# The opening of an attention and MLP kernel: products and turns in pairs of 128x64 tiles, one copy for x's second half, w_out's fields earlier

## The chip, the cores and the metric

The kernel runs on one core of a Trainium2 chip. The metric is the device time of one execution in microseconds (us). The time before is the median of three runs.

## The reference

Two blocks in a row, all in float32:

```
q_p, k_p = phi(q), phi(k)            # phi(x)[i, j] = (S1 x)[i] * (S2 x)[j], 8 x 8 features of 32 dimensions
kv = sum over tokens of k_p * v;  z = sum over tokens of k_p
x  = (q_p kv) / (q_p z + 1e-6)       # 4 batches, 4 heads, 1088 tokens, head_dim 32
x  -> (4 * 1088, 128)                # the heads of a token side by side
out = gelu(x @ w_in) @ w_out         # w_in 128 x 2048, w_out 2048 x 128, exact gelu
```

S1, S2, w_in and w_out arrive as 64-bit words. The kernel takes each apart into a low word, a mantissa field and an exponent field, and puts a float32 together from them (the class `Rounding`).

## The kernel before, in words

The 4352 tokens are taken in eight chunks of 512 (`n` = 0 to 7, two to a batch) and one of the 256 left over (`n` = 8). For each chunk there is `xT[n]`, the attention output with the 128 channels on partitions and the tokens along the row. `hidden(n, fi)` multiplies one 128-column tile of w_in with `xT[n]` into a PSUM bank (512 columns), and ScalarE applies gelu to it. There are 16 such steps for each chunk. `project(n, fi)` multiplies a gelu tile with a tile of w_out and sums in PSUM. Most chunks are projected by `two_products` instead, a scheme of seven products for eight on quarter tiles, in which two products of 64 output columns always stand side by side.

A float32 matmul is two passes in the trace, each with a weight load. The page writes the tile shape as rows*columns: 128*128 is the whole array, 128*64 one half of its columns. Two 128*64 instructions on the two halves run at the same time.

The instructions of each engine run in the order of the text: a loop at the end of the kernel makes each instruction follow the one before it on its engine. So a wait holds up all that stands behind it on that engine.

The opening, up to the first steps, is written out by hand. Chunk 0 takes x by token: `divide` (VectorE, L738) makes `x_tok` in two halves of 256 tokens, and each half is turned into `xT[0]` by TensorE against `ident` and then copied out of PSUM. The first half goes through `turn_half` (two transposes at L759 and one ScalarE copy at L760), the second through `turn_half_apart` (two transposes at L751 into two banks, one copied by ScalarE and one by VectorE, both L753). Between the two, TensorE makes one factor of chunk 1's query features (`expand_products`, L579). Then `first_hidden` starts the first products of chunk 0 by columns, as the parts of `xT[0]` come (L794). In the first four steps TensorE runs `hidden(0, 0)` to `hidden(0, 3)` (L778), the products of chunk 1's ratio (`ratio_products`, L688) and the projections of chunk 0 (L965), while VectorE and ScalarE unfold w_in's second piece and w_out's first two pieces, multiply chunk 1's features (`expand_copy` L585 on ScalarE, `expand_multiply` L590 on VectorE) and make `xT[1]` (`ratio`, L707 and L708). At step 4 `first_hidden(1, half)` starts chunk 1.

`Rounding` for one piece of weights has these parts: `fields` (VectorE: exponent field L283, mantissa field L288), `low_words` (ScalarE, L270), `exponents` (ScalarE, L294, needs the exponent field), `mantissas` (VectorE, L302, needs mantissa field and low words), `signs` (VectorE, L307, needs the exponents), `product` (L312). `finish` is mantissas, signs and product.

Two PSUM banks serve `hidden_bank` and two serve `out_bank`, each given out in turn. `hidden(n, fi)` splits its tile into two halves of 64 columns only from step 17 on (`by_halves=t >= 17`); up to there it and `project` use the whole array.

Of the kernel before, what the change touches and what calls it, by code (L numbers as in the profile page):

```python
# [8 lines left out]
FP = mybir.dt.float32  # L9
# [7 lines left out]
def kernel(  # L17
# [18 lines left out]
    pe, dve, act, pool, sp = nc.tensor, nc.vector, nc.scalar, nc.gpsimd, nc.sync  # L36
# [11 lines left out]
    CW = JC * 128  # L48
# [13 lines left out]
    att = ctx.enter_context(tc.tile_pool(name="att", bufs=2))  # L62
# [5 lines left out]
    def work_banks():  # L68

        return wps.tile([128, 2, CW], FP, name="w_ps")  # L70
# [7 lines left out]
    def hidden_bank():  # L78
        return hps.tile([128, CW], FP, name="h_ps")

    def out_bank():
        return ops.tile([128, CW], FP, name="o_ps")


    by_act, by_dve, by_pool = act.copy, dve.tensor_copy, pool.tensor_copy
# [11 lines left out]
    w_in_sb = [big.tile([d_model, c1 - c0], FP, name=f"w_in{i}") for i, (c0, c1) in enumerate(pieces)]  # L97
    w_out_sb = [big.tile([128, c1 - c0], FP, name=f"w_out{i}") for i, (c0, c1) in enumerate(pieces)]
# [42 lines left out]
    def block(dtype=U32):  # L141

        b = big.tile([128, NB, 512], U32, name="block", bufs=3)
        return b if dtype == U32 else b.bitcast(dtype)
# [82 lines left out]
    ident = big.tile([128, 128], FP, name="ident")  # L227
# [318 lines left out]
    qT, qp, xT = {}, {}, {}  # L546
# [36 lines left out]
    def expand_copy(n, i):  # L583
        A[i] = att.tile([128, 2, CW // 2], FP, name="A_sb")
        act.copy(out=A[i][:, :, :width[n] // 2], in_=B_of[n, i][:, :, :width[n] // 2])  # L585

    def expand_multiply(n, i):
        W = width[n]
        a, b = (t.rearrange("f g (r x) -> f g r x", r=2) for t in (A[i][:, :, :W // 2], B_of[n, i][:, :, W // 2:W]))
        dve.tensor_mul(out=qp[n].rearrange("f r (g x) -> f g r x", g=G)[:, 2 * i:2 * i + 2], in0=a, in1=b)  # L590
# [90 lines left out]
    def ratio_products(n, banks):  # L681

        for s in range(2):
            for c in range(NP):
                rows = slice(c * F, (c + 1) * F)
                for r in range(2):
                    for i, (h, w) in enumerate(((2 * c + r, kz_apart[rows, r, c, :D]), (2 * (1 - c) + r, z_cols[rows, r]))):
                        pe.matmul(banks[h * D:(h + 1) * D, i, s * HW:(s + 1) * HW], lhsT=w,  # L688
                                  rhs=qp[n][rows, r, s * HW:(s + 1) * HW], start=True, stop=True)
# [20 lines left out]
    x_tok = {}  # L710
# [33 lines left out]
        act.activation(out=den[:, 0], in_=by_head(bank)[:, :, D], func=ACT.Copy, bias=1e-6)  # L744
        return den

    def turn_half_apart(n, i, banks):
        if i == 0:
            xT[n] = att.tile([128, CW], FP, name="xT", bufs=3)
        for j, ps in enumerate(banks):  # L750
            pe.transpose(ps[:, :128], in_=x_tok[n, i][:, j].rearrange("p h d -> p (h d)"), identity=ident)  # L751
        for j, ps in enumerate(banks):
            (by_act, by_dve)[j](out=xT[n][:, i * 256 + j * 128:i * 256 + (j + 1) * 128], in_=ps[:, :128])  # L753

    def turn_half(n, i, ps, copy):
        if i == 0:
            xT[n] = att.tile([128, CW], FP, name="xT", bufs=3)
        for j in range(2):
            pe.transpose(ps[:, j * 128:(j + 1) * 128], in_=x_tok[n, i][:, j].rearrange("p h d -> p (h d)"), identity=ident)  # L759
        copy(out=xT[n][:, i * 256:(i + 1) * 256], in_=ps[:, :256])  # L760


    g_of, o_of = {}, {}

    def w_tile(w, fi):
        i = max(i for i, (c0, c1) in enumerate(pieces) if c0 <= fi * 128)
        at = fi * 128 - CUTS[i]
        return w[i][:, at:at + 128]

    first_banks, begun = {}, [(0, 0), (1, 0)]  # L770

    def hidden(n, fi, by_halves=False):
        W = width[n]
        ps = first_banks.pop((n, fi)) if (n, fi) in first_banks else hidden_bank()
        w = w_tile(w_in_sb, fi)
        for rows in (slice(0, 64), slice(64, 128)) if by_halves else (slice(0, 128),):
            if (n, fi) not in begun:
                pe.matmul(ps[rows, :W], lhsT=w[:, rows], rhs=xT[n][:, :W], start=True, stop=True)  # L778
        if n < NCH and fi < USUAL[n]:
            g_of[n, fi] = mlp.tile([128, CW], FP, name="g", bufs=4)  # L780
        else:
            if fi % NB == 0:
                blocks[n, fi // NB] = block(FP)
            g_of[n, fi] = blocks[n, fi // NB][:, fi % NB]
        act.activation(out=g_of[n, fi][:, :W], in_=ps[:, :W], func=ACT.Gelu)  # L785

    def first_hidden(n, half):

        if half == 0:
            first_banks[n, 0] = hidden_bank()  # L790
        parts = 1 if n else 2
        for i in range(parts):
            cols = slice(half * 256 + i * 256 // parts, half * 256 + (i + 1) * 256 // parts)
            pe.matmul(first_banks[n, 0][:, cols], lhsT=w_tile(w_in_sb, 0), rhs=xT[n][:, cols], start=True, stop=True)  # L794

# [154 lines left out]
    def project(n, fi, parts=range(B // 2), cols=slice(None)):  # L952
        first, final = fi == (BLOCKED if n == NMAIN else 0), fi == (USUAL[n] if n < NCH else NF) - 1
        if first and n not in o_of:
            o_of[n] = out_bank() if n < NMAIN else [out_bank() for i in range(B // 2)]
        g = g_of[n, fi]
        if n == NMAIN:

            for i in parts:
                for half in range(2):  # L960
                    rows, at = slice(half * 64, (half + 1) * 64), i * 128 + half * 64
                    pe.matmul(o_of[n][i][rows, :128], lhsT=g[:, at:at + 64], rhs=w_tile(w_out_sb, fi),  # L962
                              start=first, stop=final)
            return
        pe.matmul(o_of[n][:, cols], lhsT=w_tile(w_out_sb, fi), rhs=g[:, cols], start=first, stop=final)  # L965

    def store(n):
        oT = mlp.tile([128, JC, d_model], FP, name="oT")
# [42 lines left out]
    banks = [out_bank(), out_bank()]  # L1011
# [26 lines left out]
    for c in range(NP):  # L1038
        rows = slice(c * F, (c + 1) * F)
# [5 lines left out]
    w_out = [Rounding(w, beside=b) for w, b in zip(w_out_sb[:2], w_in)]  # L1045
    parts = [range(2), range(2, JC)]
# [10 lines left out]
    divide(0, nd[1:], 1, den)  # L1057
    expand_products(1, (1,))
    w_in[1].fields()
    turn_half_apart(0, 1, [out_bank(), out_bank()])  # L1060
    w_in[1].exponents()
    w_in[1].mantissas()
    w_in[1].signs()
    w_in[1].product()
    expand_copy(1, 0)
# [100 lines left out]
    def begin(w):  # L1166

        rounding[w.name] = Rounding(w)
        rounding[w.name].fields()
# [51 lines left out]
    for n in range(3, NCHUNK):  # L1221

        t = (n - 1) * NF
# [75 lines left out]
    for t in range(len(steps) + LAG):  # L1299
        if t < 4:  # L1300

            hidden(0, t)
            if t == 0:
                expand_multiply(1, 0)
                w_out[0].fields()
                expand_copy(1, 1)
                expand_multiply(1, 1)
            if t == 1:
                w_out[0].low_words()
                w_out[0].exponents()  # L1310
                w_out[0].finish()
                w_out[1].fields()
            if t == 2:
                w_out[1].low_words()
            if t == 3:
                banks = work_banks()
                ratio_products(1, banks)
                w_out[1].mantissas()
                w_out[1].exponents()
                w_out[1].signs()  # L1320
                w_out[1].product()
                turned = ratio_turn(banks)
                ratio(1, banks, turned)
                project(0, 0)
                project(0, 1)
            continue
        if t == 4:
            begin(turns[0])
            by_scalar(turns[0], *low)
            for f, *a in products[t] + products[t + 1]:  # L1330
                f(*a)
            for half in range(2):
                first_hidden(1, half)
        for n in drains[t]:
            drain(n)
        sooner = t == NMAIN * NF
        if sooner:
            for f, *a in products[t]:
                f(*a)
        if t < len(steps):  # L1340
            n, fi = steps[t]
            hidden(n, fi, by_halves=t >= 17)
        if t < len(steps) and steps[t][0] < NMAIN and steps[t][1] % NB == NB - 1:
            n, b = steps[t][0], steps[t][1] // NB
            if b >= first_block(n):
                token_sums(n, b)
        for f in slots[t]:
            f()
        for n in done[t]:
            store(n)  # L1350
        if t not in (4, 5) and not sooner:
            for f, *a in products[t]:
                f(*a)
# [41 lines left out]
```

## Time and profile before

| | |
|---|---|
| time, median of 3 runs | 257.62 us (257.45 to 257.73) |
| the profiled execution's own time | 257.87 us |
| its span, first to last instruction | 256.1 us |
| PE busy | 252.0 us (98%) |
| VectorE (DVE) busy | 158.0 us (62%) |
| ScalarE (ACT) busy | 113.7 us (44%) |
| GpSimd (POOL) busy | 176.0 us (69%) |
| `hidden`, L778 | 538 instructions, 137.0 us busy, of them 30 in the shape 128*128 |
| `project`, L965 | 24 instructions, 11.9 us busy |
| granted TensorE clock | 1.000 |

The span is that of one profiled execution, and all starts and durations below come from it. A busy time is the union of the instructions of a group, and the mean of a matmul is longer than the distance from one to the next, since matmuls overlap in the array. In the chain of work that ended last each piece is put down to what released the next one, followed back from the last instruction. In a timeline the columns are start and duration in us, engine, line, operation, output and inputs, shape and count, and in brackets the engine's idle time before it and what ended that.

### The profile page before, as it was taken

The numbers are of one execution on the slowest core, as the hardware profiler recorded it, in microseconds if no ns is written. First come the engines' busy times: TensorE is split into PE (matmuls) and PEld (weight loads), VectorE is DVE, ScalarE is ACT, GpSimd is POOL, SyncE is SP. The second block draws the span as 40 slices with busy tenths as digits, with TensorE's granted clock in tenths as the row PEclk, the third lists the DMA queues.
The fourth block names the chain that finished last, engine by engine and source line by source line (L and its number), as shares of the span: only waits on it lengthen the run. The fifth ranks groups of instructions, "written<-read, shape, count | busy, mean of one in ns | idle before, by whom it ended". The sixth has DMA issues, their size and how long they took to land.

```text
span 256.1 us, 6035 instructions
## 1 busy us (share of the span) xinstructions
PE 252.0 (98%) x2444; PEld 131.3 (51%) x2444; DVE 158.0 (62%) x333; ACT 113.7 (44%) x220; POOL 176.0 (69%) x193
## 2 busy tenths in 40 slices
PE   8999999999999999999999999999999999999994
PEld 4844444455454545454444455455544444445784
DVE  3899996949798987580178986299507000700282
ACT  3683885333535333533335332533444333532541
POOL 3516019999849787587758775787758777877960
PEclk9999999999999999999999999999999999999999
DMA  6699658710001101102000002000110200020021
GB/s 207 174 298 314 183 123 211 183 19 7 0 3 15 26 4 26 18 10 33 3 0 0 0 13 33 4 1 0 19 25 3 42 0 3 3 40 0 0 33 33
DMA packets 29083, 13.50 MB, mean 53 GB/s; under 512 B 21888, under 2 KB 27264, under 8 KB 29056
## 3 DMA queue, kind: packets, MB, share of 16 engines
q1 hardware_dynamic: 28624, 12.79, 20.4%
q8 instruction: 19, 0.31, 0.6%
q10 hardware_dynamic: 432, 0.33, 0.4%
q14 instruction: 8, 0.07, 0.1%
HBM read 10.88 MB, written 2.23 MB: 51 GB/s over the span
## 4 chain that ended last, share of the span: by engine, by line
PE 95%; DVE 3%; issue 0%; ACT 0%; DVEq 0%
PE h_ps L778 44%; PE o_ps L864 35%; PE o_ps L965 3%; PE w_ps L934 2%; PE w_ps L463 1%; PE w_ps L613 1%; PE w_ps L668 1%; PE w_ps L997 1%; PE w_ps L579 1%; PE h_ps L348 1%; PE o_ps L962 1%; PE o_ps L452 1%; PE w_ps L1084 1%; DVE bits_m L302 0%; DVE bits_e L307 0%; DVE q_pT L590 0%
## 5 line engine op out<-in xcount | busy, mean ns | idle before, releaser
L778 PE MATMUL h_ps<-xT,w_in 128*64 128x512 f32 (+2 forms) x538 | 137.0, 568 | 0.0
L785 ACT ACTIVATE block<-h_ps 128x512 f32<-128x512 f32 (+1 forms) x132 | 75.4, 572 | 119.0 <-PE h_ps L778 115.9
L864 PE MATMUL o_ps<-block,w_out 128*64 128x256 f32 x232 | 59.5, 379 | 0.0
L829 POOL TENSOR_TENSOR bits_low<-block 128x512 f32<-128x512 f32 x29 | 37.3, 1288 | 28.3 <-ACT block L785 28.3
L778 PEld LDWEIGHTS h_ps<-xT,w_in 128*64 128x64 f32 (+1 forms) x538 | 40.7, 140 | 27.1 <-issue 7.8
L864 PEld LDWEIGHTS o_ps<-block,w_out 128*64 128x64 f32 x232 | 31.7, 137 | 39.2 <-issue 28.0
L830 POOL TENSOR_TENSOR bits_a<-block 128x512 f32<-128x512 f32 x29 | 37.0, 1277 | 11.7 <-ACT block L785 11.6
L879 DVE COPY sums<-o_ps 64x256 f32<-64x256 f32 x8 | 3.3, 417 | 58.9 <-PE o_ps L864 58.9
L831 POOL TENSOR_TENSOR bits_e<-bits_a,block 128x512 f32<-128x512 f32 x29 | 37.4, 1288 | 2.3
L832 POOL TENSOR_TENSOR bits_m<-block,bits_e 128x512 f32<-128x512 f32 x29 | 37.3, 1286 | 2.3
L864 PE MATMUL o_ps<-bits_low,small 128*64 128x256 f32 x116 | 29.8, 380 | 0.0
L864 PE MATMUL o_ps<-block,small 128*64 128x256 f32 x116 | 29.8, 380 | 0.0
L864 PE MATMUL o_ps<-bits_a,small 128*64 128x256 f32 x116 | 29.8, 379 | 0.0
L864 PE MATMUL o_ps<-bits_m,w_out 128*64 128x256 f32 x116 | 29.8, 379 | 0.0
L864 PEld LDWEIGHTS o_ps<-block,small 128*64 128x64 f32 x116 | 15.7, 137 | 18.7 <-issue 10.9
L864 PE MATMUL o_ps<-bits_e,small 128*64 128x256 f32 x116 | 17.7, 384 | 0.0
L864 PEld LDWEIGHTS o_ps<-bits_m,w_out 128*64 128x64 f32 x116 | 15.9, 137 | 0.0
L864 PEld LDWEIGHTS o_ps<-bits_a,small 128*64 128x64 f32 x116 | 15.8, 137 | 0.0
L864 PEld LDWEIGHTS o_ps<-bits_low,small 128*64 128x64 f32 x116 | 15.7, 137 | 0.0
L625 DVE STREAM_TRANSPOSE w_ps<-w_ps 128x512 f32<-128x512 f32 (+1 forms) x7 | 4.8, 687 | 17.1 <-ACT xT L679 12.7
L864 PEld LDWEIGHTS o_ps<-bits_e,small 128*64 128x64 f32 x116 | 7.8, 137 | 11.5 <-issue 9.1
L1108 DVE TENSOR_REDUCE w_ps<-k_p 128x128 f32<-128x1024 f32 x6 | 11.9, 1977 | 0.2
(222 smaller groups left out, 317.6 us busy)
## 6 DMA issues: line engine op xcount, KB each, us to landing
block<-in_moe_w_in_dram SPq DMA_DIRECT2D x3, 512.0 KB, 9.7
block<-in_moe_w_out_dram SPq DMA_DIRECT2D x3, 512.0 KB, 10.1
k<-in_k_dram SPq DMA_DIRECT2D x12, 128.0 KB, 2.7
v<-in_v_dram SPq DMA_DIRECT2D x12, 128.0 KB, 3.3
q<-in_q_dram SPq DMA_DIRECT2D x24, 64.0 KB, 2.6
out_dram<-oT SPq DMA_DIRECT2D x21, 64.0 KB, 2.3
q_first<-in_q_dram SPq DMA_DIRECT2D x2, 256.0 KB, 3.9
v<-in_v_dram SPq DMA_DIRECT2D x2, 256.0 KB, 4.2
```

Of the source, the lines that this page charges most:

```text
L625: dve.transpose(out=tok, in_=ps[:, :, :H2])
L778: pe.matmul(ps[rows, :W], lhsT=w[:, rows], rhs=xT[n][:, :W], start=True, stop=True)
L785: act.activation(out=g_of[n, fi][:, :W], in_=ps[:, :W], func=ACT.Gelu)
L829: pool.tensor_sub(out=s[3], in0=a11, in1=a21)
L830: pool.tensor_add(out=s[1], in0=a21, in1=a22)
L831: pool.tensor_sub(out=s[2], in0=s[1], in1=a11)
L832: pool.tensor_sub(out=s[4], in0=a12, in1=s[2])
L864: pe.matmul(acc[n][bank][half * 64:(half + 1) * 64, col:col + HW], lhsT=fixed, rhs=moving, start=opens and e == 0 and name in "4715", stop ...
L879: dve.tensor_copy(out=N[lo, 0, one], in_=a0[lo, one])
L934: pe.matmul(acc[NMAIN][rows, COLS_REM[name]], lhsT=tokens[:, rows], rhs=fixed, start=k == 0 and name == ORDER_REM[0], stop=k == BLOCKED // ...
L965: pe.matmul(o_of[n][:, cols], lhsT=w_tile(w_out_sb, fi), rhs=g[:, cols], start=first, stop=final)
L1108: dve.tensor_reduce(out=sums[:, c], in_=k_p[b][c].rearrange("p n r f -> p (r f) n"), axis=mybir.AxisListType.X, op=AX.add)
```

## The change

Four edits, all in the opening:

- Every `hidden`, `first_hidden` and `project` works on two halves of 64 columns (`sides`), also before step 17. `first_hidden(0, half)` has one piece of 256 columns in place of two of 128.
- The turns of `x_tok` are no longer transposes: `turn_x` multiplies each half of 64 columns of x with `ident`, as an ordinary product.
- x's second half is turned into one bank and copied once, by ScalarE. The VectorE copy and one `out_bank` go.
- `w_out[0].low_words()` (ScalarE) stands ahead of that turn, and `w_out[0].fields()` (VectorE) between the mantissas and the signs of `w_in[1]`. Before, they stood in steps 1 and 0.

```diff
-    def turn_half_apart(n, i, banks):
-        if i == 0:
-            xT[n] = att.tile([128, CW], FP, name="xT", bufs=3)
-        for j, ps in enumerate(banks):
-            pe.transpose(ps[:, :128], in_=x_tok[n, i][:, j].rearrange("p h d -> p (h d)"), identity=ident)
-        for j, ps in enumerate(banks):
-            (by_act, by_dve)[j](out=xT[n][:, i * 256 + j * 128:i * 256 + (j + 1) * 128], in_=ps[:, :128])
-
     def turn_half(n, i, ps, copy):
         if i == 0:
             xT[n] = att.tile([128, CW], FP, name="xT", bufs=3)
         for j in range(2):
-            pe.transpose(ps[:, j * 128:(j + 1) * 128], in_=x_tok[n, i][:, j].rearrange("p h d -> p (h d)"), identity=ident)
+            turn_x(ps[:, j * 128:(j + 1) * 128], x_tok[n, i][:, j])
         copy(out=xT[n][:, i * 256:(i + 1) * 256], in_=ps[:, :256])
...
+    sides = (slice(0, 64), slice(64, 128))
+
+    def turn_x(to, x):
+        x = x.rearrange("p h d -> p (h d)")
+        for rows in sides:
+            pe.matmul(to[rows], lhsT=x[:, rows], rhs=ident, start=True, stop=True)
+
-    def hidden(n, fi, by_halves=False):
+    def hidden(n, fi):
...
-        for rows in (slice(0, 64), slice(64, 128)) if by_halves else (slice(0, 128),):
+        for rows in sides:
...
-        parts = 1 if n else 2
-        for i in range(parts):
-            cols = slice(half * 256 + i * 256 // parts, half * 256 + (i + 1) * 256 // parts)
-            pe.matmul(first_banks[n, 0][:, cols], lhsT=w_tile(w_in_sb, 0), rhs=xT[n][:, cols], start=True, stop=True)
+        cols = slice(half * 256, (half + 1) * 256)
+        for rows in sides:
+            pe.matmul(first_banks[n, 0][rows, cols], lhsT=w_tile(w_in_sb, 0)[:, rows], rhs=xT[n][:, cols], start=True, stop=True)
...
-        pe.matmul(o_of[n][:, cols], lhsT=w_tile(w_out_sb, fi), rhs=g[:, cols], start=first, stop=final)
+        for rows in sides:
+            pe.matmul(o_of[n][rows, cols], lhsT=w_tile(w_out_sb, fi)[:, rows], rhs=g[:, cols], start=first, stop=final)
...
     w_in[1].fields()
-    turn_half_apart(0, 1, [out_bank(), out_bank()])
+    w_out[0].low_words()
+    turn_half(0, 1, out_bank(), by_act)
     w_in[1].exponents()
     w_in[1].mantissas()
+    w_out[0].fields()
     w_in[1].signs()
     w_in[1].product()
...
             if t == 0:
                 expand_multiply(1, 0)
-                w_out[0].fields()
                 expand_copy(1, 1)
                 expand_multiply(1, 1)
             if t == 1:
-                w_out[0].low_words()
                 w_out[0].exponents()
                 w_out[0].finish()
                 w_out[1].fields()
```

In the order of each engine's instructions the change moves nothing else: GpSimd's and SyncE's orders stay as they were.

More of the change, by code (lines that the diff above doesn't have):

```diff
@@ L959, in project @@
             for i in parts:
[L960 to L963, printed above, removed]
+                tokens = g[:, i * 128:(i + 1) * 128]
+                for rows in sides:
+                    pe.matmul(o_of[n][i][rows, :128], lhsT=tokens[:, rows], rhs=w_tile(w_out_sb, fi), start=first, stop=final)
             return
-        pe.matmul(o_of[n][:, cols], lhsT=w_tile(w_out_sb, fi), rhs=g[:, cols], start=first, stop=final)
+        for rows in sides:
+            pe.matmul(o_of[n][rows, cols], lhsT=w_tile(w_out_sb, fi)[:, rows], rhs=g[:, cols], start=first, stop=final)
     def store(n):
@@ L1341 @@
             n, fi = steps[t]
-            hidden(n, fi, by_halves=t >= 17)
+            hidden(n, fi)
         if t < len(steps) and steps[t][0] < NMAIN and steps[t][1] % NB == NB - 1:
```

## The prediction

> **What bounds the kernel now.** I read the page first, its chain of work that ended last:
>
> ```profile
> ## 4 chain that ended last, share of the span: by engine, by line
> PE 95%; DVE 3%; issue 0%; ACT 0%; DVEq 0%
> ```
>
> The chain is TensorE nearly throughout, and 3% is VectorE. The same chain in order of time, from 13 to 25 us, shows where that 3% lies:
>
> ```profile
> 13.55 0.37 PE h_ps L759 x2
> 13.91 0.62 PE w_ps L579 x16
> 14.53 0.27 PE o_ps L751
> 14.80 0.02 issue
> 14.83 0.27 ACT xT L753
> 15.10 0.05 issue
> 15.15 0.41 DVE bits_m L302
> ...
> 23.56 0.44 DVE xT L708
> 24.00 0.04 issue
> 24.04 0.70 PE h_ps L794 x2
> ```
>
> From 14.8 to 24.0 us the path is VectorE: it unfolds the weights and then makes the second chunk's xT (L708). TensorE resumes the path at 24.04 with `first_hidden(1, 1)`. After that I compared the starts of successive products in the trace: from 24.6 us to the last product at 252.6 us only 2.2 us are lost, nearly all in steps of about 0.09 where the tile shape changes, none of them a wait that the first 40 us set. So the change counts in two places: when VectorE finishes xT, and how fast TensorE goes from there to 42 us, where the old kernel uses pairs already. The timelines of the engines give the prices:
>
> ```profile
> 13.48 0.44 PE L759 MATMUL h_ps<-ident,x_tok 128*128 128x128 f32 x2
> 13.85 0.69 PE L579 MATMUL w_ps<-qT,Srep 32*64 32x256 f32 x16
> 42.52 0.44 PE L421 MATMUL w_ps<-ident,k_rem 128*64 128x128 f32 x4
> 42.79 1.03 PE L778 MATMUL h_ps<-xT,w_in 128*64 128x512 f32 x4
> ...
> 13.95 0.37 ACT L760 COPY xT<-h_ps 128x256 f32<-128x256 f32 x1 [0.52 <-PE h_ps L759]
> 14.83 0.27 ACT L753 COPY xT<-o_ps 128x128 f32<-128x128 f32 x1 [0.50 <-PE o_ps L751]
> 14.99 0.51 ACT L294 ACTIVATE bits_r<-bits_e,below 128x256 uint32<-128x256 uint32 x1
> ...
> 14.94 0.29 DVE L753 COPY xT<-o_ps 128x128 f32<-128x128 f32 x1
> ...
> 15.53 0.43 DVE L307 SCALAR_TENSOR_TENSOR bits_e<-small,bits_r 128x256 uint32<-128x256 uint32 x1
> ```
>
> The reader is to see that two turns by transpose hold TensorE for 0.37 (13.48 to 13.85), that one turn by two 64-column products (L421) holds it for 0.27, and that VectorE's `signs` (L307, 15.53) starts 0.03 after ScalarE's exponents (L294) end at 15.50: that edge is tight already.
>
> **The products in pairs.** A full 512-column product takes 0.857 (L778 and L965 alternate at 27.25, 28.10, 28.96); a pair takes the same (L778 128*64: 42.79 and the next instruction 0.86 later). The 20 products between 24.6 and 42 us (17.3 / 0.857) therefore gain and lose nothing. A pair gains only where TensorE has stood still: its first pass is 0.53 long in the 128-column form (0.107 of weight load exposed, 19.60 to 20.13) and 0.05 shorter with 64 columns (L421's first pass takes 0.16, its second 0.11). Most such places lie beside VectorE's path. On the path it is `first_hidden(1, 1)`, -0.05. Behind it `hidden(1, 2)` waits 0.10 today for gelu(1, 0) to free its bank; in pairs that gelu would end near 25.63 and TensorE be through with `hidden(1, 1)` at 25.69, so the wait goes as well. Together -0.13, rounded down because the two starts nearly coincide. `first_hidden(0, ...)` needs four pair passes of 0.216 for eight of 0.111, and is not on the path.
>
> **The turns as products.** L421's four instructions are one turn, two passes of each half side by side; a second turn adds 0.21 (L493: four instructions from 59.59 to 59.80). Two turns stream for 0.27 + 0.21 = 0.48, and 0.1 goes to the change of shape behind them, 0.58 against 0.37: +0.21. There are two such pairs in series on TensorE (L759, then L579, then L751), and L751 starts when L579 is through (14.46, x_tok was ready at 14.29), so the second starts at 14.68 and its last pass, begun 0.38 later, ends 0.27 after that, at 15.34. Before, the first bank was ready at 14.79, the other at 14.90.
>
> **The copy of x's second half.** One 256-element copy by ScalarE instead of 128 by each engine. It waits for all of the turn: start 15.37, 0.37 long by L760, and the next instruction follows 0.27 after its start (0.16 behind the 128 one). VectorE loses L753: it holds 0.21 of its time (14.94 to 15.15). But the exponents stand behind this copy in ScalarE's order: they start at 15.64 rather than 14.99 and end at 16.15 rather than 15.50. VectorE's `signs` waits for them and starts at 16.19 instead of 15.53, +0.66; behind it wait the w_in product and the two L590.
>
> **w_out's fields and low words.** The fields (L283 and L288, 0.20 each) leave the place between the two L590 and run while VectorE now waits for the exponents, so 0.40 of the 0.66 comes back; without that cover they would cost as before. The low words (L270, 0.44) go into ScalarE's wait ahead of the second copy (idle 0.50 before L753, longer now), cost nothing there, and leave the stretch at 17.34. Their data landed at 13.54, before either asks.
>
> **The sum.** `signs` 16.19, w_in product 16.65, first L590 16.99, second L590 17.59 by VectorE's own order. ScalarE sets nearly the same: exponents 15.64, A copy 16.06, gelu(0, 0) 16.54 (its product ends at 16.45), second A copy 17.03 to 17.61, hence second L590 at 17.65, against 17.34: +0.31. All behind it is one queue of VectorE, so xT is ready at 24.30 for 23.99. With -0.13 on TensorE the span grows by 0.18: 256.1 + 0.2 = 256.3. The profiled execution took 257.87 for a span of 256.1, 0.25 over the median of the runs, so against the median: 257.62 + 0.18 = 257.8.
>
> Bounds of the disputed term, the turn: no dearer than the transposes (0.37), the exponents would end at 15.72, the second L590 would start near 17.15 and the sum be -0.3; if the halves of a turn ran one after the other, eight passes of 0.11, each pair of turns costs 0.65 more than now, `signs` slips to about 17.1 and the sum is +1.0. L421 and L493 are the same operation on another tile, so I stay near them.
>
> The Trainium skill, "TensorEngine Tiling (Array Packing)", Restrictions, says that column tiling does without the transpose mode for FP32, and "TensorE: Matmul & The Clock Gate", Terms, calls that mode four times faster for FP32. By the four, an estimate, the two turns would stream for some 0.87 and the sum be near +1.0; by L421 and L493 the ratio is two, and the trace speaks against the four.
>
> **Rivals.**
> - *TensorE's own queue takes VectorE's place (slower).* The gelus slip with the copy: gelu(0, 1) ends at 18.11 for 17.47 in my sum, `hidden(0, 3)` waits for its bank, and behind it stand the ratio products and eight passes of L965 (19.60 to 23.14 before, to 23.67 after), then `first_hidden(1, 0)` to 24.10. xT is due at 24.35 on TensorE. It decides once gelu(0, 1) ends 0.25 later than I have it, and if ScalarE's five instructions before it slip by 0.6 the sum is about +0.55. For it: ScalarE is without a gap from 14.8 to 20; against it: the low words have left that stretch.
> - *The turns run at a fourth of the speed (slower):* +1.0, as above.
> - *The wait does not bite (faster).* If the turns are as quick as before, VectorE keeps the 0.21 of L753 and TensorE its 0.13: -0.3. For it: the chain is VectorE's and an instruction leaves it; against it: L421's four instructions for a transpose's one.
> - *Nothing of it counts:* 0.0, if VectorE had slack ahead of 24.04. The chain shows none.
>
> **How the numbers follow.** About 0.2% (0.5 us) is what a measurement of this kernel can tell from no change. My forecast, +0.2, has 0.60 and its own range is -0.1 to +0.5; TensorE's queue 0.16, the slow turns 0.07, the faster case 0.14, nothing 0.03. Slower by over 0.2%: most of the queue case (0.12), the slow turns (0.07), a tail of the forecast (0.03), 0.22. Faster by over 0.2%: only the far end of the faster case and what I may have priced wrongly in the pairs, 0.08. The rest is 0.70. The range goes from the faster case, 257.62 - 0.4 = 257.2, to most of the slower ones, 257.62 + 0.9 = 258.5.
>
> **What would show it.** In the profile after: the second turn's eight instructions from about 14.7, ScalarE's one copy at 15.4, exponents at 15.6, VectorE idle about 0.5 before `signs` at 16.2, the two L590 0.6 apart, xT's last half near 24.3, first project after it near 26.6 (26.39 before), and from there the same distance to the end. I am wrong if `signs` starts before 15.7, if pairs take other than 0.86, or if TensorE rather than VectorE precedes 24.3.

## The result, and the profile after

The changed kernel takes 258.14 us (median of 12 runs, 257.66 to 258.56), the kernel before in the same session 257.52 us (12 runs, 257.04 to 257.78). The ratio is 1.0025 (95% interval 1.0015 to 1.0034): 0.6 us slower, where 0.2 was forecast. 257.8 was the forecast time, in a range of 257.2 to 258.5; the range holds the time, but 0.70 stood on "within 0.2%" and 0.22 on "slower by more", and it was slower by a little more. The opening went nearly as it was forecast, 0.29 us slower for 0.18. A second cost came on top, 130 us later, which no step of the forecast had.

The chain of work of the changed kernel, in order of time; the columns are start, length and what:

```profile
13.51 0.59 PE h_ps L769 x8
14.10 0.62 PE w_ps L579 x16
14.71 0.61 PE o_ps L769 x8
15.33 0.02 issue
15.35 0.37 ACT xT L752
15.72 0.42 ACT bits_r L294
16.14 0.02 issue
16.16 0.44 DVE bits_e L307
...
23.85 0.44 DVE xT L708
24.28 0.04 issue
24.33 0.65 PE h_ps L792 x4
```

Before, the chain went from the turn to VectorE within 0.6 us (L751, a copy, L302). Now it runs through the longer turn, ScalarE's copy (L752) and ScalarE's exponents (L294), and reaches VectorE at its `signs` (L307). VectorE's own timeline shows what that does to it:

```profile
15.29 0.29 DVE L283 TENSOR_SCALAR bits_e<-small 128x256 uint32<-128x256 uint32 x1
15.49 0.29 DVE L288 TENSOR_SCALAR bits_a<-small 128x256 uint32<-128x256 uint32 x1
16.16 0.43 DVE L307 SCALAR_TENSOR_TENSOR bits_e<-small,bits_r 128x256 uint32<-128x256 uint32 x1 [0.38 <-ACT bits_r L294]
...
16.97 1.33 DVE L590 TENSOR_TENSOR q_pT<-A_sb,w_ps 128x512 f32<-128x512 f32 x2
```

The bracket at 16.16 is the new wait. w_out's fields (15.29 and 15.49) fill the first part of it, and the two L590 now stand together. In the kernel before, the fields stood between them:

```profile
16.34 0.68 DVE L590 TENSOR_TENSOR q_pT<-A_sb,w_ps 128x512 f32<-128x512 f32 x1
16.93 0.28 DVE L283 TENSOR_SCALAR bits_e<-small 128x256 uint32<-128x256 uint32 x1
17.14 0.28 DVE L288 TENSOR_SCALAR bits_a<-small 128x256 uint32<-128x256 uint32 x1
17.34 0.68 DVE L590 TENSOR_TENSOR q_pT<-A_sb,w_ps 128x512 f32<-128x512 f32 x1
```

Step by step, against the forecast (us from the span's start):

| step | before | forecast | after |
|---|---|---|---|
| second turn, start and last end | 14.46, 14.90 | 14.68, 15.34 | 14.64, 15.30 |
| exponents end | 15.50 | 16.15 | 16.13 |
| `signs` | 15.53 | 16.19 | 16.16 |
| second L590 | 17.34 | 17.65 | 17.62 |
| xT ready | 23.99 | 24.30 | 24.27 |
| first project behind xT | 26.39 | 26.6 | 26.64 |
| from there to the last product | 226.22 | as before | 226.66 |

The span's first 13.4 us, which the change leaves alone, end up to 0.85 us sooner or later from one execution to the next (first turn at 12.63 to 13.48 in two traces of the kernel before), so traces are compared from the first turn on: the first project comes 12.91 and 12.92 after it in the two traces before, 13.20 and 13.20 in two after. The opening costs 0.29.

The last row is the second cost. TensorE stands still once near 156 us, in the last of three stretches in which a batch's sums, its sketches and an attention share a few microseconds:

```profile
155.79 0.65 PE L862 MATMUL o_ps<-bits_e,small 128*64 128x256 f32 x4
156.67 0.65 PE L777 MATMUL h_ps<-xT,w_in 128*64 128x512 f32 x2 [0.23 <-issue]
```

The same two groups in the kernel before, without the wait:

```profile
155.53 0.65 PE L864 MATMUL o_ps<-bits_e,small 128*64 128x256 f32 x4
156.01 1.03 PE L778 MATMUL h_ps<-xT,w_in 128*64 128x512 f32 x4
```

"issue" means that the engine waited for nothing that the profile shows. From the first product of this stretch (the sum over keys, L463) to the hidden product behind it the trace before has 3.63 us, this one 4.03.

### The profile page after: what moved, and what is told of

It is laid out like the page before. It is cut to its first block, busy times and chain, and to the rows that moved or that the text cites. A ratio compares the mean times of both kernels' runs of the same rounds, so it can differ in the third digit from the quotient of the medians.

```text
span 256.8 us, 6176 instructions
## 1 busy us (share of the span) xinstructions
PE 252.5 (98%) x2514; PEld 130.4 (51%) x2514; DVE 157.9 (61%) x332; ACT 114.0 (44%) x220; POOL 176.6 (69%) x193
## 4 chain that ended last, share of the span: by engine, by line
PE 95%; DVE 3%; issue 0%; ACT 0%; DVEq 0%
PE h_ps L777 44%; PE o_ps L862 34%; PE o_ps L963 3%; PE w_ps L932 2%; PE w_ps L463 1%; PE w_ps L613 1%; PE w_ps L668 1%; PE w_ps L995 1%; PE w_ps L579 1%; PE h_ps L348 1%; PE o_ps L960 1%; PE o_ps L452 1%; PE w_ps L1084 1%; DVE q_pT L590 1%; DVE bits_e L307 0%
## 5 line engine op out<-in xcount | busy, mean ns | idle before, releaser
L777 PE MATMUL h_ps<-xT,w_in 128*64 128x512 f32 (+1 forms) x568 | 137.4, 569 | 0.2 <-issue 0.2
L777 PEld LDWEIGHTS h_ps<-xT,w_in 128*64 128x64 f32 x568 | 40.1, 137 | 28.3 <-issue 8.4
## 6 DMA issues: line engine op xcount, KB each, us to landing
q_first<-in_q_dram SPq DMA_DIRECT2D x2, 256.0 KB, 3.9
v<-in_v_dram SPq DMA_DIRECT2D x2, 256.0 KB, 4.2
```

## The experiments

Each kernel was run beside the kernel before. "Burst" is the stretch just named: 329 TensorE instructions (weight loads and matmuls) in 3.63 us, 91 a microsecond against 19 on the mean of the span. The theories: **A**, the turns as products make the copy late, the copy ScalarE's exponents, and these VectorE. **F** (called B in the expectations of the first four runs), TensorE's added instructions shift the places at which its instruction supply is refilled, and in the burst it can run dry. Rival to both: the pairs themselves cost, or the extra 0.4 was chance.

**The two kernels again.** `c_before` and `c_after` are the two kernels unchanged.

> The kernel before once more, for a second trace of it. All theories: ratio 1.000. What is asked is how far TensorE's record differs between two executions of one program: first project behind xT near 26.4 us, and from 24.6 us to the last product no wait of TensorE over 0.15 us, as in the first trace. A stall of 0.3 us or more somewhere in the steady part would show that such stalls come and go by themselves.

> The changed kernel once more. Theory A (the opening alone: exponents queued behind the slower turn): first project behind xT near 26.65 as in its first trace, +0.26 us, and no stall of TensorE at 156.7 us, which was chance; time +0.1% to +0.15%. Theory B (the added TensorE instructions move the places where its instruction supply runs dry): the stall of about 0.4 us at 156.7 us is there again, and the time is +0.25%.

`c_before`: 0.9994 (0.9983 to 1.0005), first project 12.92 after the first turn, burst 3.63. `c_after`: 1.0022 (1.0011 to 1.0034), first project 13.20, burst 3.63. So the opening's 0.29 repeats and the stall does not always come. The spans tell the rest: the 93 executions of the kernel before that ran beside the experiments have 255.1 to 256.1 (mean 255.65); 23 of the changed kernel 255.5 to 256.8 (mean 256.13), 5 of them over 256.4, which is the highest of before and the opening's 0.3. Neither theory as put: the stall is a matter of some executions.

**The turns alone.**

```diff
-            pe.transpose(ps[:, :128], in_=x_tok[n, i][:, j].rearrange("p h d -> p (h d)"), identity=ident)
+            turn_x(ps[:, :128], x_tok[n, i][:, j])
...
-            pe.transpose(ps[:, j * 128:(j + 1) * 128], in_=x_tok[n, i][:, j].rearrange("p h d -> p (h d)"), identity=ident)
+            turn_x(ps[:, j * 128:(j + 1) * 128], x_tok[n, i][:, j])
```

`turn_x` is that of the changed kernel; the two banks and the two copies stay.

> Before, with the turns of x as products and nothing else (two banks and two copies stay). Theory A: second turn from 14.68, its banks ready at 15.11 and 15.34, the VectorE copy at 15.38, signs at 15.92 (15.53 before), all of VectorE behind it +0.39, since no fields fill the wait: +0.4 us, +0.15%. Theory B: 12 matmuls more of 2444, no great move of the supply: the same +0.4 at most. If the turns do not matter: 0.

1.0017 (1.0006 to 1.0028). `signs` 0.39 later than before, as forecast, but the first project 0.53 later (13.44). Its chain shows 15.31 for VectorE's late copy and no fields to fill the wait:

```profile
...
14.67 0.61 PE o_ps L750 x8
15.28 0.02 issue
15.31 0.04 DVE xT L758
15.34 0.17 issue
15.52 0.41 DVE bits_m L302
```

The turns alone cost more than the whole change does in the opening: the other edits give some of it back.

**The pairs alone.** `hidden`, `first_hidden` and `project` as in the change, turns, copies and fields as before.

> Before, with hidden, first_hidden and project in pairs and nothing else. Theory A: VectorE's path is as before, TensorE gains 0.05 in first_hidden(1, 1) and 0.1 before hidden(1, 2): -0.13 us, -0.05%. Theory B (58 matmuls more, so the places of the supply move as in the changed kernel): +0.2 to +0.4 us, with a stall of TensorE in the steady part.

1.0002 (0.9993 to 1.0011). First project 12.93 (12.91 before; 0.13 less was expected), burst 3.63, 12 spans from 255.2 to 256.0. The pairs cost nothing. They also give nothing: xT comes 0.11 later, since `first_hidden(0, 1)` in one piece makes gelu(0, 0) 0.17 later and the low words behind it hold VectorE's mantissas, and TensorE wins that back behind xT.

**The change without the turns.**

```diff
 def turn_x(to, x):
     x = x.rearrange("p h d -> p (h d)")
-    for rows in sides:
-        pe.matmul(to[rows], lhsT=x[:, rows], rhs=ident, start=True, stop=True)
+    pe.transpose(to, in_=x, identity=ident)
```

> The changed kernel with the turns as transposes again (turn_x is one transpose); all else as changed. Theory A (turns, hence copy, hence exponents): second turn through at 1.42 us after the first one's start, the copy 1.46, exponents end at 2.24, signs 2.28 (2.06 before, 2.72 in the changed kernel), second L590 at 3.71 (3.86 before, 4.18 changed); first project behind xT 0.1 us ahead of before, 0.4 ahead of the changed kernel: ratio 0.9995. Theory F (TensorE now and then runs out of instructions in a burst near 156 us, where its fetches fall in the changed kernel): 24 instructions fewer ahead of the burst, fetches as in the kernel with pairs alone, no executions with a span over 256.0. If the pairs and not the turns were the cost: ratio 1.001 to 1.002.

0.9995 (0.9985 to 1.0005). `signs` at 2.28 after the first turn and the second L590 at 3.73, as expected; first project at 12.75, 0.16 ahead of before and 0.45 ahead of the changed kernel. Burst 3.63, 11 spans from 255.2 to 255.9. Together with the last two runs this is theory A for the opening: the turns are the cost, and the other edits are worth 0.16.

**The exponents ahead of the copy, then the whole order of ScalarE.**

```diff
-    w_out[0].low_words()
-    turn_half(0, 1, out_bank(), by_act)
     w_in[1].exponents()
+    w_out[0].low_words()
+    turn_half(0, 1, out_bank(), by_act)
```

> The changed kernel with w_in[1].exponents() ahead of w_out's low words and of the second copy of x. Theory A, strict (only the exponents are late): signs at 2.26 after the first turn's start, VectorE's path 0.3 us shorter than in the changed kernel, time as before. Theory A2 (ScalarE's whole order is late: the second A copy stands behind gelu(0, 0), which waits for the copied half): signs early, but the second L590 at 4.2 as in the changed kernel, and no gain: +0.3 us over before. Theory F: TensorE's program is that of the changed kernel, so about one execution in three has a span 0.2 to 0.6 above the others, which adds 0.1 to 0.2 to the mean.

1.0036 (1.0020 to 1.0051). `signs` early (2.25), the second L590 at 4.19, first project at 13.24: A2. VectorE's wait has moved to the A copy, which stands behind gelu(0, 0):

```profile
16.42 0.68 DVE L590 TENSOR_TENSOR q_pT<-A_sb,w_ps 128x512 f32<-128x512 f32 x1
17.56 0.69 DVE L590 TENSOR_TENSOR q_pT<-A_sb,w_ps 128x512 f32<-128x512 f32 x1 [0.46 <-ACT A_sb L585]
```

The second kernel also puts `expand_copy(1, 1)` ahead of gelu(0, 0) and `w_out[0].exponents()` ahead of gelu(0, 1).

> As the kernel with the exponents first, and also the second A copy ahead of gelu(0, 0) and w_out[0]'s exponents ahead of gelu(0, 1). Theories A and A2: nothing on VectorE's path waits for ScalarE now; second L590 at 3.65 after the first turn's start, xT at 10.3 (10.5 before, 10.83 changed); TensorE's projections end no sooner than before, so the first project is at 12.95, as before: ratio 1.000. If the second L590 is early and xT is not, the price lay elsewhere. Theory F: some spans 0.2 to 0.6 above the others, as in the changed kernel.

1.0039 (1.0025 to 1.0053). The second L590 is at 3.65, as expected, and xT at 10.87, not at 10.3. This was my miss: the wait moved once more, to w_out's second piece, whose exponents stand behind gelu(0, 3), and that gelu's product waits for the bank of gelu(0, 1):

```profile
19.73 0.43 DVE L307 SCALAR_TENSOR_TENSOR bits_e<-small,bits_r 128x256 uint32<-128x256 uint32 x1 [0.49 <-ACT bits_r L294]
```

So a late turn shifts the gelus, and moving ScalarE's other work ahead of them only moves the place where VectorE meets the delay. Both kernels have the changed kernel's TensorE program, and both show the stall: burst 4.12 and 3.74, 11 of 23 spans over 256.4, up to 257.9.

**The place of the fetches.** `keep_busy(8, bank, 112)` for `keep_busy(2, bank, 448)` at the very start puts 24 TensorE instructions more ahead of everything.

> The changed kernel with the warm-up at the start as eight products of 112 columns instead of two of 448: 12 matmuls and 12 weight loads more ahead of everything, same length. Theory A: opening as in the changed kernel, +0.3 us. Theory F: every fetch of TensorE's instructions falls 24 instructions earlier in the work, so the stall near 156 us goes away or another comes; the spread of the spans (0.8 between the fast and the late start of the inputs) loses its tail above 256.3. If the tail is not of the fetches, it stays: 3 to 5 of 12 over 256.3.

1.0070 (1.0057 to 1.0084). The opening is the changed kernel's (13.19), the burst takes 4.93, and all five spans lie from 257.2 to 257.8. The stall grew instead of going away:

```profile
154.35 0.97 PE L613 MATMUL w_ps<-qT,S_abc 64*32 64x256 f32 x19
156.08 0.64 PE L613 MATMUL w_ps<-qT,S_abc 64*32 64x256 f32 x8 [0.76 <-issue]
```

That the place counts and not the opening is asked of the old kernel:

```diff
-    keep_busy(2, bank, 448)
+    keep_busy(1, bank, 448)
+    small_noughts = [nc.const_aps.tensor(0.0, [128, m], FP) for m in (64, 16)]
+    for i in range(42):
+        pe.matmul(bank[i % 2 * 64:(i % 2 + 1) * 64, CW - 16:], lhsT=small_noughts[0], rhs=small_noughts[1], start=True, stop=True)
```

> The kernel before with 164 TensorE instructions more at the very start (one warm-up product of 448 columns and 42 tiny ones of 64x16 in place of two of 448), nothing else. In number ahead of the last batch's burst that is the changed kernel with the other warm-up (165 more than before). Theory F (TensorE runs out of instructions where a fetch falls into the burst): from the burst's first product to the hidden products behind it 4.5 to 5 us instead of 3.63, time +1.0 to +1.5 us, ratio 1.004 to 1.006, though the opening behind the warm-up is the old one. If the stall belongs to the changed opening: 3.63 and ratio 1.000.

1.0213 (1.0192 to 1.0235). The time can't be used: the tiny products ran longer than the warm-up that they replace, and the first turn starts at 16.94. Behind that the opening is the old one (first project 12.91 after the turn) and the burst takes 4.64, with the same wait in the same line:

```profile
157.99 0.97 PE L613 MATMUL w_ps<-qT,S_abc 64*32 64x256 f32 x20
159.44 0.63 PE L613 MATMUL w_ps<-qT,S_abc 64*32 64x256 f32 x7 [0.48 <-issue]
```

Then in the other direction, first with `project` on the whole array (48 instructions fewer than the changed kernel).

> The changed kernel with project on the whole array again: 48 TensorE instructions fewer ahead of the burst, the same columns streamed. Theory A: opening as in the changed kernel, first project 13.2 us after the first turn (12.91 before). Theory F: the burst's distance is 3.63 in every execution, so the spans are those of before plus 0.3: none over 256.4, mean +0.3, ratio 1.001 (1.0022 and 1.0025 in the changed kernel). If the stall comes from anything but the count: ratio 1.002 and a tail over 256.4 in a third of the executions.

1.0116 (1.0099 to 1.0132). The burst is 3.63 again, but the kernel is 3 us slower for a reason that I had overlooked: `hidden` in halves and `project` on the whole array alternate, and each change of shape costs.

```profile
26.18 1.13 PE L962 MATMUL o_ps<-g,w_out 128*128 128x512 f32 x2
27.24 1.08 PE L777 MATMUL h_ps<-xT,w_in 128*64 128x512 f32 x4
28.25 1.13 PE L962 MATMUL o_ps<-g,w_out 128*128 128x512 f32 x2
```

A hidden and a project product start 2.07 apart here (26.18 to 28.25) and 1.71 in the kernel before (26.39 to 28.10). From the first project to the next batch's features (L1084) it is 18.24 us for 15.54: 2.7 us for eight projects with two changes of shape each, 0.17 for a change. The Trainium skill, "TensorEngine Tiling (Array Packing)", Key Properties, says that a change of the tiling mode drains the engine; this trace agrees in so far as each change costs time, 0.17 us here.

The last run takes the halves back only beside VectorE's path (`hidden(0, 1)` to `hidden(0, 3)` and the four projections ahead of `first_hidden(1, 0)`): 28 instructions fewer.

> The changed kernel with seven products beside VectorE's path (hidden(0, 1) to hidden(0, 3) and the four projections before first_hidden(1, 0)) on the whole array again: 28 TensorE instructions fewer ahead of the last burst. Theory A: the opening stays that of the changed kernel or gets up to 0.2 worse, since two more changes of shape fall into TensorE's reserve: first project 13.2 to 13.4 us after the first turn. Theory F: burst to hidden 3.63 again and no tail of the spans: highest span at most 0.3 to 0.5 over the highest of before, spread as in before; the mean span is up by the opening alone, 0.3 to 0.5. If the tail is not of the instruction count, a third of the spans lie 0.2 to 0.6 above the rest and the burst can be longer.

1.0016 (1.0006 to 1.0027). First project at 13.27, burst 3.63, 12 spans from 255.5 to 256.4, mean 255.98: 0.33 over the mean of before, which is the opening's 0.35 of its own trace and nothing else.

| TensorE instructions ahead of the burst | kernels | burst in the trace | instruction 3266 starts, us into the burst | spans over 256.4 |
|---|---|---|---|---|
| 2796 and 2820 | before (twice), turns alone | 3.63 | 14.19, 14.20; 12.24 | 0 of 105 (with those of `c_before`); 1 of 8 (256.5, with an opening 0.5 later) |
| 2889 | `e_project_whole` | 3.63 | 6.87 | not comparable; 258.4 to 259.0 |
| 2908 to 2914 | `e_short`, pairs alone, change without turns (twice) | 3.63 | 5.78, 5.14, 5.14, 5.14 | 0 of 47 |
| 2937 | changed (twice), `e_exp_first`, `e_order` | 4.03, 3.63, 4.12, 3.74 | 4.03, 3.48, 4.12, 3.74 | 16 of 46 |
| 2960 and 2961 | `e_before_pad`, `e_pad` | 4.64, 4.93 | 3.59, 3.88 | 5 of 5 of `e_pad` |

That the stall hangs on this number and not on the opening is shown: `e_pad`, `e_short` and the changed kernel have openings within 0.1 us of each other and other bursts, and `e_before_pad` has the old opening. The traces also show why 24 instructions decide. Counted from the start of the span (weight loads, matmuls and the few semaphore instructions in the trace, as in the first column), all five traces with a stall wait at the same instruction of TensorE: 3265 others start before it, and the fourth column has its start. It belongs to a hidden product (L777) in three of them and to a sketch (L613) in two, so it is its place in the sequence that counts. In the changed kernel this place is the end of the burst, where the instruction ahead of it starts at 3.42; in the two padded kernels it is earlier in the burst, behind 2.74; with 2914 instructions or fewer ahead it falls behind the burst, and nothing waits there. In the second trace of the changed kernel the instruction comes 0.06 later than its like in `e_short` (3.48 for 3.42), with no cost.

That this is the supply of instructions is inferred: the profile names no wait; the trace has packets of 16 KB on the queue of kind "instruction", 19 for some 4900 TensorE instructions, one per 260. In the changed kernel one begins 1.22 us into the burst and lands at 2.58, and the stall ends at 4.03. In all five traces the stall ends 1.3 to 1.6 us after such a packet has landed. In the pairs alone one begins at 1.40 and nothing stalls, since the burst is over at 3.63 and instruction 3266 is not due before 5.14. What a packet holds, and why there is over 1 us between its landing and the end of the stall, no trace shows.

**The version that points ahead.** The change without the turns, once more.

> The changed kernel with transposes, once more, for a narrower interval: by its trace it is 0.16 us ahead of before, 0.06%. Expected 0.9990 to 1.0000; no stall in the burst.

0.9991 (0.9981 to 1.0001). First project at 12.75 again, burst 3.63, 12 spans from 255.1 to 255.9. By both traces it is 0.16 us faster than the kernel before and 0.45 faster than the changed one. Its mean spans lie 0.14 and 0.18 below those of the kernel before beside it, but the intervals of both times include no change, so against the kernel before the times do not settle it.

## Why the prediction was right, and what it lacked

- **What bounds the kernel.** As forecast: VectorE to xT, then TensorE with no reserve. All of xT's delay but 0.03 reached the first project in both traces.
- **The turns.** Forecast from L421 and L493: 0.58 for 0.37, second turn 0.22 later, its last end 0.44 later. The trace after has them at those places, counted from the first turn (1.21 to 1.86, for 0.99 to 1.42). The rule of the Trainium skill ("TensorE: Matmul & The Clock Gate", Terms) that would have made them four times as long is not what this trace shows: two turns take four passes side by side in place of two, 0.58 us in place of 0.37.
- **The copy and the exponents.** Forecast +0.66 for `signs`; measured 0.67 from the first turn (2.73 for 2.06). Fields and low words cost nothing where they went, as forecast, and the second L590 is 0.32 later (4.18 for 3.86), forecast 0.31.
- **The products in pairs, 0.86 each.** Right: from the first project to L1084 15.55 for 15.54.
- **The term of -0.13 behind xT was mis-sized.** It measured -0.03. Its first part came: `first_hidden(1, 1)` holds the chain for 0.65 where it was 0.70. The second did not: gelu(1, 0) waits for two semaphores in the changed kernel, ScalarE's own among them, and starts 0.11 after its product (25.09 for 24.98) instead of 0.04, so `hidden(1, 2)` still waits for its bank. In the pairs alone this gelu waits for one semaphore, and the term is -0.09 (xT to first project 2.31 for 2.40).
- **The sum.** 0.18 forecast, 0.29 measured for the opening. The step that failed is "and from there the same distance to the end". The burst near 156 us adds, on the mean, what is left between the opening and the mean of the spans, 0.48 - 0.29 = 0.19. About 0.08 more lies outside the span (time less span is 1.88 on the mean of 23 runs, 1.80 before); no run explains that, and `e_exp_first` and `e_order`, with the same TensorE program, have 1.80 and 1.79. That the range holds the time is in part luck: its upper end was put there for TensorE's own queue and for slow turns, and neither came.
- **The rivals.** TensorE's own queue did not bind: its projections ended in time, and the first half of chunk 1's first product started at 23.65, forecast 23.67. The faster case is what the kernel without the turns does, at half the price put on it (-0.16 for -0.3).

## What to carry to other kernels

Where two engines hand work back and forth in a fixed order, price a slower step by what is queued behind its consumer: each of the two pairs of turns cost TensorE 0.22 us, and VectorE's `signs`, which uses nothing of x, came 0.45 later by them (2.73 for 2.28 with transposes), because ScalarE's exponents stand behind the copy of x. Moving that instruction ahead does not help as long as the chain itself is late; the wait turns up at the next hand-over.
Keep the tile shape of a stretch the same throughout, and after a change that adds instructions to a saturated engine look at its densest bursts in several executions, also far from the edit.

## What the runs showed of the hardware that was not expected

- TensorE stalls of 0.1 to 1.3 us, named "issue", in a burst of 329 instructions in 3.63 us, present or absent by the number of TensorE instructions ahead of it, and with the same program in some executions and not in others. The wait stands at the same place of TensorE's instruction sequence in all five traces that have it, behind 3265 instructions, whatever instruction that is.
- 0.17 us for each change between whole-array and half-array products of 512 columns where the two alternate. At two single changes in the kernel before, the next shape starts 0.95 and 0.96 after a product of 0.86 (40.98 to 41.93 and 151.42 to 152.38).
- The time to the first turn differs by up to 0.85 us between executions of one program, so that single traces can be compared only from a common point on.
